# A planner's model of a shared PSUM bank, of DMA landing and of a shared port is altered, and its shifts are drawn anew

## The chip, the cores and the metric

The kernel runs on one core of one Trainium2 chip. The metric is the device time of one execution in microseconds (us). The engines are PE (matrix multiply), DVE (VectorE), ACT (ScalarE), POOL (GpSimd) and SP, which here only issues DMAs. Each engine works through its own instructions strictly in their order and waits for the others through semaphores.

## The reference, cut to what matters

```python
# attention, 4 batches, 8 heads, 1152 keys, head size 64; q pooled in pairs: 576 queries
q_pool = q.reshape(B, H, S // 2, 2, D).mean(axis=3)
scores = scale * np.matmul(q_pool, k.transpose(0, 1, 3, 2))
attn = np.exp(scores - np.max(scores, axis=-1, keepdims=True))
attn = attn / (np.sum(attn, axis=-1, keepdims=True) + 1e-09)
x = np.matmul(attn, v)                       # -> 2304 tokens x 512
# first feed-forward layer, 512 -> 2048 -> 512, a rational function between
h = x @ w_in
g = (a[0] + a[1]*h + a[2]*h*h + a[3]*h*h*h) / (1 + abs(b[0])*abs(h) + abs(b[1])*h*h + 1e-6)
x = g @ w_out
# second layer: one of 8 experts for each token, 512 -> 1024 -> 512
e_idx = np.argmax(x @ w_gate, axis=1)
out[mask] = gate_w * sigmoid * (np.maximum(x[mask] @ w1[e], 0.0) @ w2[e])
```

## The kernel before

Every float32 operand is split into a high and a low float16 part, and a product is three matmuls. The work runs in two stages. In the second, the experts' slots of 128 tokens are written out by hand in a fixed order; the diff does not touch it. In the first, a **planner** (`Plan`) sets the order. The code calls `plan.add` for every step with a key (its wanted place), the engines that may do it with a cost in us for each, and the names that it reads and writes. `Plan.order` then places all steps one after another on a model of the five engines: at each turn it takes, over all engines, the ready step with the earliest start (ties go by key), and so it decides both the order on each engine and, where two engines may do a step, which one does. `SHIFT` holds a number for each kind of step that is added to its key; `BIAS` and `PEN` hold numbers that make an engine dearer for steps with a choice. A kind ends in "." for the start of the program and in "!" for its end. The program that comes out has the fixed order; the costs exist only in the model.

Attention is done in 144 units of 128 query rows each (one head, or two heads of half a tile). Unit n goes through these steps: the scores for keys 0 to 1023 into the PSUM tile `sab` and those for the last 128 keys into a part of the PSUM tile `shared` (L828, PE; L825 for half tiles); the maximum over `sab` (L838, DVE) and over the rest (L841, DVE, called mc in the code); the exponent's bias (L848 on ACT or L850 on DVE, a step with a choice); the two exponentials (L856, ACT); the high part of the result (L865 on ACT or L867 on DVE), the low part (L871, mostly POOL); a transpose of both by DMA (L873, SP) into one of two buffers `pt`; the product with v into another part of `shared` (L880, PE). After four units a short chain on DVE reads the sums (L635) and writes the result out of `shared` (L909). The tile `shared` is one PSUM bank: the scores' rest, the products, and small sums across partitions lie in it side by side.

18 tiles of 128 tokens then go through the first feed-forward layer in four groups each: 48 matmuls with w_in (L1172 to L1174), the rational function on ACT, DVE and POOL (L1183 to L1206), 12 with w_out (L1213 to L1215). A chain of small steps chooses the expert (`route`). Before all that, both weight matrices are loaded as 8-byte numbers (L971), made float32 on DVE (L974 to L981), scaled and split (L1028, L651). `chain` adds each small instruction on DVE as a step of its own; `scale_of` makes the exponent's scale and `gate` the token's weight, each beginning with an instruction that reads two SBUF operands.

The model in `Plan.order` knows: for a step with `bank` on `shared`, PE waits until readers have finished and readers wait until PE has; for a step with `port`, DVE and POOL exclude each other; a DMA's result is ready when its modelled transfer ends plus `LAT["SP"]`.

Of the kernel before, what the change touches and what calls it, by code (L numbers as in the profile page):

```python
# [21 lines left out]
SHIFT = {'X/PE': -98.7,
 'X/PE.': -1.1,
 'bias/DVE+ACT': 54.5,
 'bias/DVE+ACT!': -16.9,
 'bias/DVE+ACT.': 35.7,
 'chain cf/DVE': -8.9,
 'chain cf/DVE.': 22.0,
 'chain den/DVE': -3.4,
 'chain den/DVE!': -27.4,  # L30
 'chain den/DVE.': -30.2,
 'chain esc/DVE': 53.8,
 'chain esc/DVE!': -67.3,
 'chain esc/DVE.': -212.0,
 'chain ps/DVE': 37.4,
 'chain ps/DVE!': 3.7,
 'chain qsc/DVE': -65.4,
 'chain qsc/DVE.': 3.5,
 'chain ro/DVE': 1.0,
 'chain ro/DVE!': -13.3,  # L40
 'chain rt/DVE': -12.9,
 'chain rt/DVE!': 0.1,
 'chain sc/DVE': 0.5,
 'chain sc/DVE.': -4.9,
 'chain wsi/DVE.': -4.5,
 'chain wso/DVE.': -0.9,
 'chain xm/DVE': 18.4,
 'chain xm/DVE.': 25.9,
 'chain xs/DVE': 44.6,
 'chain xt/DVE': -9.5,  # L50
 'chain xt/DVE.': -97.6,
 'chain yg/DVE': 0.5,
 'chain yg/DVE!': -1.3,
 'const/DVE.': -42.6,
 'cwld/SP.': 49.7,
 'first/DVE': 6.5,
 'firstn/DVE': 20.6,
 'gh/ACT': -36.3,
 'gh/ACT!': 0.1,
 'gh/DVE': -20.5,  # L60
 'gl/DVE': -68.3,
 'gl/DVE!': -44.3,
 'gw/DVE': 4.9,
 'gw/SP': 35.1,
 'h/ACT': -231.3,
 'h/DVE': 18.2,
 'h/PE': -0.1,
 'h/PE.': 306.2,
 'kT/SP': -4.3,
 'kT/SP.': 229.4,  # L70
 'kr/SP': 91.6,
 'kr/SP.': -7.0,
 'krB/SP.': 182.2,
 'line/PE': 40.5,
 'line/PE.': 23.8,
 'mab/DVE': 62.8,
 'mab/DVE!': -18.0,
 'mab/DVE.': -42.5,
 'mc/DVE': -1.1,
 'mc/DVE!': -113.7,  # L80
 'mc/DVE.': 242.3,
 'mk/ACT': -19.4,
 'mk/ACT.': 6.6,
 'mk/DVE': 3.3,
 'most/PE': 3.4,
 'most/PE.': -63.0,
 'mv/DVE': 28.4,
 'mv/DVE.': -28.4,
 'mxi/DVE.': -105.4,
 'mxo/DVE.': 23.3,  # L90
 'nB/DVE+ACT.': 4.9,
 'nBl/DVE+POOL.': -79.2,
 'nrm/DVE+ACT': -24.2,
 'nrm/DVE+ACT.': -145.8,
 'nrmQ/DVE': 7.3,
 'nrmQ/DVE+ACT': 291.9,
 'nrmQl/DVE+POOL': 101.6,
 'nrmQl/DVE+POOL.': 43.8,
 'nrml/DVE+POOL': -5.1,
 'nrml/DVE+POOL.': -100.6,  # L100
 'oacc/POOL+DVE': -226.7,
 'oacc/POOL+DVE!': 167.8,
 'p/ACT': 127.7,
 'p/ACT!': 31.0,
 'p/ACT.': 109.5,
 'pad/SP': 13.0,
 'pad/SP.': -32.6,
 'padded/SP!': 8.8,
 'pads/SP': 86.8,
# [1 line left out]
 'pc/ACT!': -7.3,
 'pc/ACT.': -4.2,
 'ph/DVE': -0.9,
 'ph/DVE+ACT': 5.4,
 'ph/DVE+ACT!': 272.0,
 'pl/POOL+DVE': -9.0,
 'pl/POOL+DVE!': 6.3,
 'pl/POOL+DVE.': -68.5,
 'pt/SP': 1.2,
 'pt/SP!': -1.0,  # L120
 'pt/SP.': -37.0,
 'pv/PE': -51.8,
 'pv/PE!': 179.5,
 'pv/PE.': -4.0,
 'qT/SP': -24.6,
 'qm/DVE': -2.4,
 'qm/DVE.': 28.7,
 'qr/SP': -18.8,
 'qr/SP.': 2.3,
 'qs/DVE+POOL': 4.0,  # L130
 'qs/DVE+POOL.': 58,
 'raw/SP.': -2.4,
 'rawz/SP!': -120.8,
 're/ACT': -4.0,
 're/ACT!': 25.6,
 'rs/ACT': 56.2,
 'rs/ACT!': -2.3,
 'run/DVE': 38.7,
 'run/DVE!': 13.4,
 'sab/PE': -56.3,  # L140
 'sab/PE!': 69.2,
 'sab/PE.': 6.8,
 'scr/DVE.': -36.5,
 'sq/ACT.': 79.7,
 'sq/DVE': -5.5,
 'sum/PE': -19.2,
 'sum/PE!': 6.6,
 'sum/PE.': 2.8,
 'tab/DVE!': 27.1,
 'th/ACT': 5.7,  # L150
 'th/ACT!': -126.8,
 'th/DVE': -41.8,
 'tp/DVE': 26.6,
 'tp/POOL+DVE': 1.9,
 'tp/POOL+DVE!': -21.6,
 'tq/ACT': -3.5,
 'tq/ACT!': -95.6,
 'tq/DVE': 4.3,
 'tw/DVE': 54.6,
 'tw/DVE!': -77.7,  # L160
 'vh/DVE+ACT': -79.8,
 'vh/DVE+ACT.': -29.3,
 'vl/DVE+POOL': -12.4,
 'vl/DVE+POOL.': -29.5,
 'vr/SP': 11.2,
 'vr/SP.': 435.7,
 'vrB/SP.': 27.7,
 'wih/ACT+DVE.': 27.9,
 'wil/POOL+DVE.': -0.9,
 'wm/DVE!': -3.5,  # L170
 'woh/ACT+DVE.': 610.7,
 'wol/POOL+DVE.': -13.5,
 'wp/DVE!': 20.1,
 'wq/DVE!': 4.3,
 'xT/DVE': 83.2,
 'xT/SP': 85.5,
 'xT/SP!': 5.2,
 'xT/SP.': -14.1,
 'xh/DVE': 1.3,
 'xh/DVE+ACT': -66.3,  # L180
 'xh/DVE+ACT!': 72.5,
 'xh/DVE+ACT.': -8.4,
 'xhf/DVE': -23.3,
 'xl/POOL+DVE': 3.6,
 'xl/POOL+DVE!': 16.3,
 'xl/POOL+DVE.': 79.8,
 'xr/DVE': -1.8,
 'xr/DVE!': -26.4,
 'xr/DVE.': 15.4,
 'xr/POOL.': 9.0,  # L190
 'y/PE': 83.3,
 'y/PE!': 37.1,
 'y/PE.': 78.5,
 'yT/DVE': -71.4,
 'yT/DVE+ACT': -2.9,
 'yT/DVE+ACT!': 128.8,
 'yr/ACT': -227.4,
 'yr/ACT!': -8.8,
 'ysort/POOL': 10.7,
 'ysort/POOL!': -92.5,  # L200
 'yt/POOL': 34.7,
 'yt/POOL!': 0.6,
 'yz/PE': 24.1,
 'yz/PE!': 18.9,
 'zh/ACT+DVE!': 0.6,
 'zhh/ACT!': 40.0,
 'zhl/DVE!': 20.2,
 'zl/DVE+POOL!': 57.5,
 'zm/DVE!': 16.3,
 'zob/ACT!': 1.8,  # L210
 'zout/POOL!': -0.7,
 'zr/SP!': -54.0,
 'zs/DVE!': -152.9,
 'zxT/SP!': 2.2,
 'zxh/ACT+DVE!': 49.6,
 'zxl/DVE!': 8.6}
BIAS = {('bias/DVE+ACT', 'ACT'): -1,
 ('bias/DVE+ACT', 'DVE'): -1,
 ('bias/DVE+ACT!', 'ACT'): -0.7,
 ('bias/DVE+ACT.', 'ACT'): 0.26,  # L220
# [49 lines left out]
 ('vl/DVE+POOL.', 'POOL'): 140.95,  # L270
 ('wih/ACT+DVE.', 'ACT'): 3.52,
 ('wih/ACT+DVE.', 'DVE'): 38.15,
 ('wil/POOL+DVE.', 'DVE'): 1.13,
 ('wil/POOL+DVE.', 'POOL'): 45.06,
 ('woh/ACT+DVE.', 'ACT'): 2.54,
 ('woh/ACT+DVE.', 'DVE'): 23.85,
 ('wol/POOL+DVE.', 'DVE'): -0.82,
 ('xh/DVE+ACT', 'ACT'): 6.14,
 ('xh/DVE+ACT', 'DVE'): 142.52,
 ('xh/DVE+ACT!', 'ACT'): -0.87,  # L280
 ('xh/DVE+ACT!', 'DVE'): 13.33,
 ('xh/DVE+ACT.', 'ACT'): 1.59,
 ('xh/DVE+ACT.', 'DVE'): 32.01,
 ('xl/POOL+DVE', 'POOL'): 163.04,
 ('xl/POOL+DVE!', 'DVE'): -0.95,
 ('xl/POOL+DVE!', 'POOL'): 85.78,
 ('xl/POOL+DVE.', 'DVE'): 33.11,
 ('xl/POOL+DVE.', 'POOL'): 1.33,
 ('yT/DVE+ACT', 'ACT'): 47.8,
 ('yT/DVE+ACT', 'DVE'): -1,  # L290
 ('yT/DVE+ACT!', 'ACT'): -0.38,
 ('yT/DVE+ACT!', 'DVE'): 10.2,
 ('zh/ACT+DVE!', 'ACT'): 30.31,
 ('zh/ACT+DVE!', 'DVE'): -0.62,
# [1539 lines left out]
```

## Time and profile before

| | us |
|---|---|
| runs | 1262.81, 1266.67, 1269.29 (median 1266.67) |
| profiled execution, its own time | 1264.07 |
| its span, first to last instruction | 1262.2 |
| PE busy | 984.2 (78%) |
| DVE busy | 925.8 (73%) |
| ACT busy | 866.6 (69%) |
| POOL busy | 634.8 (50%) |

The mean granted clock of PE over the span is 0.922. Busy shares are means over very different stretches: the first 112 us are loads and conversion of weights, from about 173 to 950 us attention and the first layer run side by side, and from about 1085 us on only the second stage is left.

### The profile page before, as it was taken

Reading aid. Unit: us, or ns where it says so; the run is one execution under the profiler, and the core shown is the slowest. Engines: PE = TensorE matmul, PEld = TensorE weight load, DVE = VectorE, ACT = ScalarE, POOL = GpSimd, SP = SyncE. Lnnn points to the kernel's source line nnn. Section 1 sums busy time; section 2 is a strip of 40 time slices with the busy share of each in tenths; the row PEclk is TensorE's granted clock in tenths of the full one; section 3 lists DMA queues with packets and bytes.
Section 4 is the critical chain, followed back from the end, with each engine's and each line's share of the span. In section 5 each row is a group of like instructions: output and inputs, shape, how many; then the busy total and the mean of one; then the engine's idle time right before and its main releaser. Section 6 shows DMA issues by size and latency. Waiting matters only on the chain. (4 is left out here: it accounts for less than half of the span.)

```text
span 1262.2 us, 30785 instructions
## 1 busy us (share of the span) xinstructions
PE 984.2 (78%) x12212; PEld 690.9 (55%) x12213; DVE 925.8 (73%) x1950; ACT 866.6 (69%) x1326; POOL 634.8 (50%) x413
## 2 busy tenths in 40 slices
PE   0124567878778888878878887988998799899986
PEld 0002345656455565555556655766666686677763
DVE  6797856777997977889878789877777894233354
ACT  3347678988678988877888987999898561122213
POOL 0105767566576755866766774776576200000000
PEclk9966689989889999998989998999899899999988
DMA  8986699769689968687987988897765621323351
GB/s 311 250 260 137 137 189 169 125 132 194 141 156 213 165 130 154 133 184 147 174 158 132 167 181 155 152 210 129 122 109 92 189 56 51 84 74 78 77 174 29
DMA packets 493097, 186.84 MB, mean 148 GB/s; under 512 B 454179, under 2 KB 472611, under 8 KB 492836
## 3 DMA queue, kind: packets, MB, share of 16 engines
q1 hardware_dynamic: 489972, 175.22, 69.6%
q0 software_dynamic: 2960, 9.46, 2.1%
q8 instruction: 99, 1.62, 0.5%
q14 instruction: 66, 0.54, 0.1%
HBM read 61.41 MB, written 12.88 MB: 59 GB/s over the span
## 5 line engine op out<-in xcount | busy, mean ns | idle before, releaser
L871 POOL TENSOR_TENSOR att<-att 128x1152 f16<-128x1152 f32 x96 | 232.0, 2418 | 122.7 <-ACT att L865 107.1
L1172 PE MATMUL hps<-scr,winh 128*128 128x128 f16 x1152 | 216.2, 225 | 23.4 <-DVE scr L1187 19.7
L1173 PE MATMUL hps<-scr,winh 128*128 128x128 f16 x1152 | 216.3, 225 | 0.0
L1174 PE MATMUL hps<-scr,winl 128*128 128x128 f16 x1152 | 216.2, 225 | 0.0
L838 DVE TENSOR_REDUCE small<-sab 128x1 f32<-128x1024 f32 x144 | 175.3, 1218 | 54.5 <-PE sab L828 40.4
L880 PE MATMUL shared<-att 128*128 128x65 f16 (+3 forms) x4320 | 159.0, 202 | 69.4 <-DMA att<-att 46.8
L880 PEld LDWEIGHTS <-att 128*128 128x128 f16 (+1 forms) x4320 | 147.8, 106 | 103.5 <-DMA att<-att 60.9
L1187 POOL TENSOR_TENSOR scr<-scr 128x512 f32<-128x512 f32 x135 | 176.3, 1307 | 52.1 <-ACT scr L1193 28.9
L856 ACT ACTIVATE att<-sab,small 128x1024 f32<-128x1024 f32 x144 | 173.9, 1209 | 0.5
L828 PE MATMUL sab<-att 128*128 128x512 f16 x512 | 146.2, 415 | 12.2 <-ACT att L856 9.2
L828 PEld LDWEIGHTS <-att 128*128 128x128 f16 x768 | 74.1, 105 | 128.4 <-issue 73.2
L1173 PEld LDWEIGHTS <-winh 128*128 128x128 f16 x1152 | 116.2, 101 | 38.5 <-issue 26.1
L1183 DVE SCALAR_TENSOR_TENSOR scr<-scr,small,hps 128x512 f32<-128x512 f32 x144 | 106.6, 740 | 31.8 <-ACT hps L1197 16.4
L1172 PEld LDWEIGHTS <-winh 128*128 128x128 f16 x1152 | 117.4, 102 | 19.8 <-issue 4.3
L871 POOL TENSOR_TENSOR scr<-att,scr 128x1152 f16<-128x1152 f32 x39 | 95.1, 2439 | 47.6 <-ACT scr L865 39.9
L1174 PEld LDWEIGHTS <-winl 128*128 128x128 f16 x1152 | 116.5, 101 | 0.0
L1213 PE MATMUL yps<-wouth,scr 128*128 128x512 f16 x288 | 111.7, 388 | 2.3 <-ACT small L1332 2.2
L1486 PE MATMUL sab<-att 128*128 128x128 f16 x608 | 107.8, 223 | 6.4 <-ACTq L1737 3.4
L1215 PE MATMUL yps<-wouth,scr 128*128 128x512 f16 x288 | 111.6, 387 | 0.8 <-DVE small L635 0.5
L1214 PE MATMUL yps<-woutl,scr 128*128 128x512 f16 x288 | 111.7, 388 | 0.0
L1488 PE MATMUL sab<-att 128*128 128x128 f16 x608 | 107.7, 223 | 3.9 <-DVEq L1737 3.2
L1510 POOL DMA_INDIRECT out_dram<-att x19 | 18.8, 990 | 179.2 <-ACTq L1737 92.2
(211 smaller groups left out, 2440.2 us busy)
## 6 DMA issues: line engine op xcount, KB each, us to landing
att<-in_k_dram SPq DMA_DIRECT2D x16, 576.0 KB, 4.5
att<-in_q_dram SPq DMA_DIRECT2D x16, 512.0 KB, 4.5
att<-in_moe_w_dram SPq DMA_DIRECT2D x4, 2048.0 KB, 8.2
att<-in_v_dram SPq DMA_DIRECT2D x14, 576.0 KB, 4.0
woutl<-in_moe_w_in_dram SPq DMA_DIRECT2D x10, 512.0 KB, 9.6
woutl<-in_moe_w_out_dram SPq DMA_DIRECT2D x10, 512.0 KB, 4.4
att<-ysort SPq DMA_DIRECT2D x19, 257.0 KB, 2.7
wouth<-in_moe_w_in_dram SPq DMA_DIRECT2D x6, 512.0 KB, 6.4
```

The source lines that it names most:

```text
L828: T.matmul(dst[:, d0:d0 + w], qT[:, H * x + 2 * i + t, :], rhs, start=(x == 0), stop=(x == 1))
L838: A(key - ahead - .6, {"DVE": 1.13}, lambda e: V.reduce_max(mm[:, 0, bi:bi + 1], ab, axis=AX.X), r=[f"sab{par}"] + mt, w=[f"mab{n}"] + ([f ...
L856: return lambda e: S.activation(dst, src, AF.Exp, bias=mm[:, 2, bi:bi + 1], scale=esc[:, 0, i:i + 1])
L871: lambda e: eng(e).tensor_tensor(out=phs[pb][:, 1], in0=p32, in1=ph(), op=SUB),
L880: T.matmul(pvb[p0:p0 + w, bi, 0:d], pt[:, lhs, p0:p0 + w], rhs[:, h, c, :], start=(c == 0 and lhs == 0 and rhs is vh), stop=(lhs == 2 * KC ...
L1172: T.matmul(hp, wh, xh[:, kc, :], start=(kc == 0), stop=False)
L1173: T.matmul(hp, wh, xl[:, kc, :], start=False, stop=False)
L1174: T.matmul(hp, wl, xh[:, kc, :], start=False, stop=(kc == KD - 1))
L1187: return lambda e: eng(e).tensor_tensor(out=out_, in0=i0, in1=i1, op=op)
L1213: T.matmul(yps, a, wouth[:, ff, :], start=(ff == 0), stop=False)
L1214: T.matmul(yps, a, woutl[:, ff, :], start=False, stop=False)
L1215: T.matmul(yps, b_, wouth[:, ff, :], start=False, stop=(ff == KF - 1))
```

## The change

The model is altered in five places. A step on the shared bank now starts only when every other engine's steps on it, in the order in which the planner places them, have ended (one owner at a time, readers of two engines included). A DMA's result is ready 1.15 us after its modelled end, not 0.6. The chains `scale_of` and `gate` are marked as users of the port. The cost of mc is 0.27, not 0.35. In `TU` the penalties for steps with a choice go from 1.999 to 0 on DVE (`pd`), from 0 to 0.367 on ACT (`pa`) and from 1.53 to 0.548 on POOL (`pp`). With that, all of `SHIFT` and `BIAS` have new numbers. No step's arithmetic differs; the two programs issue the same steps in another order and, for steps with a choice, partly on another engine.

```diff
- 'pc/ACT': -110.8,
+ 'pc/ACT': -53.6,
...
- ('bias/DVE+ACT', 'ACT'): -1,
- ('bias/DVE+ACT', 'DVE'): -1,
+ ('bias/DVE+ACT', 'ACT'): 77.89,
+ ('bias/DVE+ACT', 'DVE'): 0.24,
...
-    LAT = {"PE": 0.2, "DVE": 0.14, "ACT": 0.17, "POOL": 0.08, "SP": 0.6}
+    LAT = {"PE": 0.2, "DVE": 0.14, "ACT": 0.17, "POOL": 0.08, "SP": 1.15}
...
-        dma = read_end = write_end = 0.0
+        dma, banked = 0.0, dict.fromkeys(engines, 0.0)
...
                     if ops[i][6]:
-                        s = max(s, read_end if e == "PE" else write_end)
+                        s = max([s] + [banked[x] for x in engines if x != e])
...
             if o[6]:
-                if e == "PE":
-                    write_end = max(write_end, end + self.LAT[e])
-                else:
-                    read_end = max(read_end, end + self.LAT[e])
+                banked[e] = end + self.LAT[e]
...
-    def chain(key, fn, r=(), w=(), after=(), bank=0):
+    def chain(key, fn, r=(), w=(), after=(), bank=0, port=0):
...
-              w=[f"esc{r}_{i}" for i in range(c.start, c.stop)])
+              w=[f"esc{r}_{i}" for i in range(c.start, c.stop)], port=1)
...
-        A(key - ahead - .4, {"DVE": 0.35},
+        A(key - ahead - .4, {"DVE": 0.27},
...
-        chain(key + .15, gate, r=[f"rs{o}", f"re{o}", "yr"], w=["yg"])
+        chain(key + .15, gate, r=[f"rs{o}", f"re{o}", "yr"], w=["yg"], port=1)
```

Line numbers of the changed kernel are smaller by 6 in the rows below (its L867 is L873 of before, L844 is L850, L835 is L841, L832 is L838, L965 is L971, L874 is L880).

**The SP queue near the end of the weights' loads.** `woutl` and `wouth` serve as buffers for the raw w_out here; L658 are transposes of k, and L873 those of a unit's exponentials. Before:

```order
L971 DMA woutl<-in_moe_w_out_dram 128x1024 x2
L658 DMA_TRANSPOSE att<-att 128x18x128
L971 DMA wouth<-in_moe_w_out_dram 128x1024 x2
L971 DMA woutl<-in_moe_w_out_dram 128x1024 x4
L971 DMA wouth<-in_moe_w_out_dram 128x1024 x2
L971 DMA woutl<-in_moe_w_out_dram 128x1024 x2
L665 DMA att<-in_k_dram 128x2x576
L658 DMA_TRANSPOSE att<-att 128x18x128
L873 DMA_TRANSPOSE att<-att 128x18x128 x2
L667 DMA att<-in_v_dram 128x2x576
```

And now:

```order
L965 DMA wouth<-in_moe_w_out_dram 128x1024 x2
L867 DMA_TRANSPOSE att<-att 128x18x128
L965 DMA woutl<-in_moe_w_out_dram 128x1024 x2
L711 DMA att<-in_q_dram 128x8x128
L965 DMA woutl<-in_moe_w_out_dram 128x1024 x2
L652 DMA_TRANSPOSE att<-att 128x18x128
L867 DMA_TRANSPOSE att<-att 128x18x128
L652 DMA_TRANSPOSE att<-att 128x8x128
L867 DMA_TRANSPOSE att<-att 128x18x128 x2
L965 DMA wouth<-in_moe_w_out_dram 128x1024 x2
L867 DMA_TRANSPOSE att<-att 128x18x128
L965 DMA woutl<-in_moe_w_out_dram 128x1024 x2
```

The last loads of w_out stood ahead of the first unit's transpose; now five transposes of units stand between them, and the queue is in order.

**DVE in the middle of the run**, some units with a group of the first layer among them. Before:

```order
L841 TENSOR_SCALAR small<-shared,small 128x128
L1187 TENSOR_TENSOR scr<-hps_78,scr 128x512
L838 TENSOR_REDUCE small<-sab_75 128x1
L867 CAST att<-att 128x1152
L841 TENSOR_SCALAR small<-shared,small 128x128
L635 SCALAR_TENSOR_TENSOR small<-shared,small 128x4
L635 RECIPROCAL small<-small 128x4
L838 TENSOR_REDUCE small<-sab_74 128x1
L909 TENSOR_TENSOR att<-shared,small 128x256
L1183 SCALAR_TENSOR_TENSOR scr<-scr,small,hps_77 128x512
L841 TENSOR_SCALAR small<-shared,small 128x128
L850 TENSOR_SCALAR small<-small 128x1
```

And now:

```order
L629 TENSOR_SCALAR small<-shared 128x1
L629 TENSOR_SCALAR small<-small 128x1 x2
L1177 SCALAR_TENSOR_TENSOR scr<-scr,small,hps_78 128x512
L835 TENSOR_SCALAR small<-shared,small 128x128
L844 TENSOR_SCALAR small<-small 128x1
L832 TENSOR_REDUCE small<-sab_74 128x1
L1177 SCALAR_TENSOR_TENSOR scr<-scr,small,hps_78 128x512
L835 TENSOR_SCALAR small<-shared,small 128x128
L1321 COPY scr<-yps 128x512
L844 TENSOR_SCALAR small<-small 128x1
L1181 TENSOR_TENSOR hps_78<-scr,hps_78 128x512
```

Before, three maxima L841 stand here with one bias L850; the other biases were on ACT. Now each L835 is followed one or two rows later by an L844, the bias, on DVE. Over the program DVE has 120 of the 144 biases, and had 42.

**PE ahead of the product of unit 130.** Before, with the scores of unit 133 (`sab`) and four transposes of the router ahead of it:

```order
L880 MATMUL shared<-att 128x65
L828 LDWEIGHTS att
L828 MATMUL sab_75<-att 128x512
L828 LDWEIGHTS att
L828 MATMUL sab_75<-att 128x512
L828 LDWEIGHTS att
L828 MATMUL sab_75<-att 128x512
L828 LDWEIGHTS att
L828 MATMUL sab_75<-att 128x512
L1324 MATMUL yps<-ident,yr 128x128 x4
L880 LDWEIGHTS att
L880 MATMUL shared<-att 128x65
```

And now, where the scores up to unit 136 and more groups of the first layer (the last rows of one stand first here) have been placed ahead of the same product:

```order
L1167 LDWEIGHTS winh
L1167 MATMUL hps_78<-scr,winh 128x128
L1168 LDWEIGHTS winl
L1168 MATMUL hps_78<-scr,winl 128x128
L1292 LDWEIGHTS tri
L1292 MATMUL yps<-oh_89,tri 128x8
L1293 LDWEIGHTS ones_82
L1293 MATMUL yps<-oh_90,ones_82 128x8
L874 LDWEIGHTS att
L874 MATMUL shared<-att 128x65
L874 LDWEIGHTS att
L874 MATMUL shared<-att 128x64
```

The product of unit 130 has moved down past PE work of later units and of the first layer.

## Rows read from the trace of the kernel before

**Rows 1.** The view by windows: columns as in its first line.
```profile
core 0: us, PE busy (x) PEld busy (x) DVE busy (x) ACT busy (x) POOL busy (x), PEclk, DMA share, GB/s
0.00:112.00 112.00, 24.15 (x63) 7.56 (x64) 89.78 (x169) 49.05 (x53) 19.79 (x19) 0.85 0.83 243
112.00:173.00 61.00, 33.40 (x408) 21.65 (x408) 44.13 (x91) 41.80 (x53) 42.24 (x22) 0.64 0.87 171
173.00:950.00 777.00, 648.67 (x8700) 459.75 (x8693) 630.31 (x1357) 665.55 (x1058) 523.67 (x329) 0.94 0.85 156
950.00:1085.00 135.00, 120.70 (x1360) 89.00 (x1359) 95.64 (x211) 68.02 (x115) 33.55 (x27) 0.95 0.39 94
1085.00:1262.00 177.00, 157.26 (x1694) 112.96 (x1692) 65.95 (x125) 42.21 (x50) 15.59 (x17) 0.95 0.33 85
```

**Rows 2.** Who waited for whom on PE, 173 to 950: total us, times, longest us.
```profile
PE shared L880 <- DMA att<-att: 34.6, 26, 3.4
...
PE shared L828 <- ACT att L856: 18.4, 19, 2.0
...
PE shared L880 <- DMA att<-scr: 18.0, 9, 6.4
```

**Rows 3.** Timeline of PE: two products that waited.
```profile
249.52 1.00 PE L880 MATMUL shared<-att 128*128 128x65 f16 x27 [0.76 <-DMA att<-att]
...
899.66 1.00 PE L880 MATMUL shared<-att 128*128 128x65 f16 x27 [2.14 <-DMA att<-att]
```

**Rows 4.** The SP queue's own waits, whole run, same columns.
```profile
SPq L873 <- PE shared L880: 49.5, 24, 7.6
```

**Rows 5.** DMA issues: count, median us from issue to landing.
```profile
att<-att SPq DMA_TRANSPOSE x137, 4.8
...
att<-scr SPq DMA_TRANSPOSE x62, 5.3
```

**Rows 6.** Who waited for whom on DVE, 173 to 950.
```profile
DVE small L635 <- ACT att L856: 3.9, 6, 1.0
...
DVE att L909 <- ACT att L856: 3.5, 5, 1.4
```

**Rows 7.** Who waited for whom on ACT, 173 to 950.
```profile
ACT small L848 <- DVE small L841: 25.4, 23, 4.2
...
ACT att L856 <- DVE small L635: 7.5, 8, 1.9
```

**Rows 8.** Groups by line and form: count, busy us, mean ns, idle before.
```profile
L841 DVE TENSOR_SCALAR_CACHE_REDUCE small<-shared,small 128x128 bf16<-128x128 f32 x144 | 49.7, 345 | 34.0 <-PE shared L828 15.5 <-PE shared L880 14.9 <-PE shared L825 1.6
...
L635 DVE SCALAR_TENSOR_TENSOR small<-small 128x1 f32<-128x1 f32 x18 | 12.7, 706 | 0.6 <-ACT small L1335 0.3 <-ACT small L1332 0.2
...
L841 DVE DVE_READ_ACCUMULATOR small<-shared,small 128x1 f32 x144 | 11.8, 82 | 0.0
...
L850 DVE TENSOR_SCALAR small<-small 128x1 f32<-128x1 f32 x42 | 8.8, 209 | 0.7
...
L635 DVE SCALAR_TENSOR_TENSOR small<-small 128x2 f32<-128x2 f32 x16 | 8.5, 538 | 0.0
...
L635 DVE SCALAR_TENSOR_TENSOR small<-shared,small 128x4 f32<-128x4 f32 x36 | 5.6, 155 | 7.7 <-PE shared L880 5.2 <-ACT att L856 2.4 <-PE shared L828 0.2
...
L848 ACT ACTIVATE small<-small 128x1 f32<-128x1 f32 x102 | 40.0, 392 | 34.8 <-DVE small L841 34.4
```

**Rows 9.** Timeline of the start, DVE, SP and PE: start us, us.
```profile
99.26 0.34 DVE L841 TENSOR_SCALAR_CACHE_REDUCE small<-shared,small 128x128 bf16<-128x128 f32 x1
...
90.42 0.80 SPq L971 DMA_DIRECT2D woutl<-in_moe_w_out_dram  x2
...
109.23 6.12 SPq L873 DMA_TRANSPOSE att<-att  x2
...
173.22 0.22 PE L1172 MATMUL hps<-scr,winh 128*128 128x128 f16 x1
...
173.83 0.22 PE L1174 MATMUL hps<-scr,winl 128*128 128x128 f16 x1
```

More of the change, by code (lines that the diff above doesn't have):

```diff
@@ L20 @@
 EARLY, LATE = 9.0, 128.0
 DIGITS = str.maketrans("", "", "0123456789_")
[L22 to L109, printed above, removed]
- 'pc/ACT': -110.8,
[L111 to L216, printed above, removed]
@@ new lines @@
+BIAS = {('bias/DVE+ACT', 'ACT'): 77.89,
+ ('bias/DVE+ACT', 'DVE'): 0.24,
+ ('bias/DVE+ACT!', 'ACT'): -0.45,
+ ('bias/DVE+ACT!', 'DVE'): 12.76,
+ ('bias/DVE+ACT.', 'ACT'): 0.32,
+ ('bias/DVE+ACT.', 'DVE'): 1.41,
+ ('nB/DVE+ACT.', 'ACT'): 0.08,
+ ('nBl/DVE+POOL.', 'DVE'): 0.17,
+ ('nBl/DVE+POOL.', 'POOL'): 0.18,
+ ('nrm/DVE+ACT', 'ACT'): 1.76,
+ ('nrm/DVE+ACT', 'DVE'): 25.14,
+ ('nrm/DVE+ACT.', 'ACT'): 0.89,
+ ('nrm/DVE+ACT.', 'DVE'): 26.67,
+ ('nrmQ/DVE+ACT', 'ACT'): -1,
+ ('nrmQ/DVE+ACT', 'DVE'): 1.05,
+ ('nrmQ/DVE+ACT.', 'ACT'): 0.53,
+ ('nrmQ/DVE+ACT.', 'DVE'): 22.22,
+ ('nrmQl/DVE+POOL', 'DVE'): -0.26,
+ ('nrmQl/DVE+POOL', 'POOL'): 7.4,
+ ('nrmQl/DVE+POOL.', 'POOL'): 1.32,
+ ('nrml/DVE+POOL', 'DVE'): -0.24,
+ ('nrml/DVE+POOL', 'POOL'): 0.36,
+ ('nrml/DVE+POOL.', 'DVE'): 215.85,
+ ('nrml/DVE+POOL.', 'POOL'): 62.52,
+ ('oacc/POOL+DVE', 'DVE'): 0.23,
+ ('oacc/POOL+DVE', 'POOL'): 28.29,
+ ('oacc/POOL+DVE!', 'DVE'): -1,
+ ('oacc/POOL+DVE!', 'POOL'): 28.54,
+ ('ph/DVE+ACT', 'ACT'): 0.84,
+ ('ph/DVE+ACT', 'DVE'): 1.39,
+ ('ph/DVE+ACT!', 'ACT'): -0.16,
+ ('ph/DVE+ACT!', 'DVE'): -1,
+ ('ph/DVE+ACT.', 'ACT'): -1,
+ ('ph/DVE+ACT.', 'DVE'): -0.11,
+ ('pl/POOL+DVE', 'DVE'): -0.16,
+ ('pl/POOL+DVE', 'POOL'): -0.86,
+ ('pl/POOL+DVE!', 'DVE'): 0.14,
+ ('pl/POOL+DVE!', 'POOL'): -0.85,
+ ('pl/POOL+DVE.', 'DVE'): 20.08,
@@ L270 @@
[L270 to L294, printed above, removed]
+ ('qs/DVE+POOL', 'POOL'): 10.94,
+ ('qs/DVE+POOL.', 'DVE'): 16.01,
+ ('qs/DVE+POOL.', 'POOL'): 1.08,
+ ('tp/POOL+DVE', 'DVE'): 72.64,
+ ('tp/POOL+DVE', 'POOL'): 0.04,
+ ('tp/POOL+DVE!', 'DVE'): 91.92,
@@ new lines @@
+ ('tp/POOL+DVE!', 'POOL'): -0.71,
+ ('vh/DVE+ACT', 'ACT'): -0.36,
+ ('vh/DVE+ACT', 'DVE'): -1,
+ ('vh/DVE+ACT.', 'ACT'): -1,
+ ('vh/DVE+ACT.', 'DVE'): -0.25,
+ ('vl/DVE+POOL', 'DVE'): -0.69,
+ ('vl/DVE+POOL', 'POOL'): 26.85,
+ ('vl/DVE+POOL.', 'DVE'): 3.38,
+ ('vl/DVE+POOL.', 'POOL'): 30.08,
+ ('wih/ACT+DVE.', 'ACT'): 0.79,
+ ('wih/ACT+DVE.', 'DVE'): 134.86,
+ ('wil/POOL+DVE.', 'DVE'): 0.14,
+ ('wil/POOL+DVE.', 'POOL'): 0.56,
+ ('woh/ACT+DVE.', 'ACT'): 50.03,
+ ('woh/ACT+DVE.', 'DVE'): 54.51,
+ ('wol/POOL+DVE.', 'POOL'): 0.85,
@@ new lines @@
+ ('xh/DVE+ACT', 'ACT'): -0.02,
+ ('xh/DVE+ACT', 'DVE'): -1,
+ ('xh/DVE+ACT!', 'ACT'): 0.04,
+ ('xh/DVE+ACT!', 'DVE'): -0.25,
+ ('xh/DVE+ACT.', 'ACT'): 20.05,
+ ('xh/DVE+ACT.', 'DVE'): 9.23,
+ ('xl/POOL+DVE', 'DVE'): -0.3,
+ ('xl/POOL+DVE', 'POOL'): 0.27,
+ ('xl/POOL+DVE!', 'DVE'): -0.96,
+ ('xl/POOL+DVE!', 'POOL'): -0.26,
+ ('xl/POOL+DVE.', 'DVE'): -0.42,
+ ('xl/POOL+DVE.', 'POOL'): 7.01,
+ ('yT/DVE+ACT', 'ACT'): 0.43,
+ ('yT/DVE+ACT', 'DVE'): 35.84,
+ ('yT/DVE+ACT!', 'ACT'): 25.21,
+ ('yT/DVE+ACT!', 'DVE'): 2.34,
@@ L295 @@
+ ('zh/ACT+DVE!', 'ACT'): -1,
+ ('zh/ACT+DVE!', 'DVE'): 1.33,
  ('zl/DVE+POOL!', 'DVE'): -1,
- ('zl/DVE+POOL!', 'POOL'): 40.87,
- ('zxh/ACT+DVE!', 'ACT'): -0.31}
+ ('zxh/ACT+DVE!', 'ACT'): 0.01}
 class Plan:
-    LAT = {"PE": 0.2, "DVE": 0.14, "ACT": 0.17, "POOL": 0.08, "SP": 0.6}
+    LAT = {"PE": 0.2, "DVE": 0.14, "ACT": 0.17, "POOL": 0.08, "SP": 1.15}
     PEN = {"PE": 0.0, "DVE": TU["pd"], "ACT": TU["pa"], "POOL": TU["pp"], "SP": 0.0}
@@ L636, in chain @@
                      r=list(r) + ([name + str(x - 1)] if x else []), w=[name + str(x)] + (list(w) if last else []),
-                     after=list(after) + list(w) if x == 0 else (), kind="chain " + list(w)[0].translate(DIGITS), bank=bank)
+                     after=list(after) + list(w) if x == 0 else (), kind="chain " + list(w)[0].translate(DIGITS), bank=bank, port=port)
     def hi(out_, in_, sc):
```

240 lines of the change are left out of this document (190 added, 50 removed).

## The prediction

> **What bounds the kernel now.** I read the view by windows first, then who waited for whom on each engine in the long middle stretch, then the groups by line. In [rows 1] the reader is to see that no engine is full in any stretch. PE's work is the same in both programs, so the time is PE's busy time plus PE's idle time. PE's idle time is 87.9 us up to 112 us (112 less 24.15), 27.6 up to 173, 128.3 up to 950, 14.3 up to 1085 and 19.7 after. The last stretch is not touched. The first is bound by loads and by DVE, which converts the weights (89.8 of 112 us). So a gain must come from the 128.3 us in the middle or from the two stretches before it. In the middle PE is busy 648.7 of 777 us, DVE 630.3, ACT 665.6: three engines between 81 and 86%, which wait for each other in turn. The longest of PE's waits there is for the DMA transpose ahead of a unit's product with v: 34.6 and 18.0 us in 35 waits, 1.5 us each; next is 18.4 us for ACT's exponential to leave `shared` [rows 2].
>
> **Term 1, the later landing.** A transpose takes 4.8 us from issue to landing in the median, 5.3 from the second buffer area [rows 5]. The model counted 1.35 + 2.65 + 0.6 = 4.6 from the issue when the queue is free; now 5.15. So the old plan placed products too early by a few tenths, and the new one about right. What that does is read from the order: for each of the units 24 to 135 I add up PE's matmuls between the end of its scores and its product, at 55.5 ns for 128 columns (twelve matmuls from 173.22 to 173.83 [rows 9]). Before it is 14.8 us in the mean, now 16.35. The products' waits of before, from the one at 249.52 to that at 899.66 [rows 3], 47.3 us for these 112 units, sort by that amount: 22 units under 12 us waited 0.77 us in the mean, 20 between 12 and 14 waited 0.44, 32 to 16 waited 0.38, 22 to 18 waited 0.28, 16 above waited 0.20. The new order has 7, 21, 31, 21 and 32 units in these classes, which makes 38.7 us: **-8.6 us**. Below, a shift of 1.6 us ends each of the 35 waits of 1.5 us: -52.6. Above, a later product frees its `pt` buffer later, and 24 transposes already waited 49.5 us on the queue for that [rows 4]: 24 x 1.6 = +38 if all of it came back to PE.
>
> **Term 2, one owner of the bank.** DVE and ACT wait for each other at `shared` though both only read: DVE's chains and results 3.9 and 3.5 us for ACT's exponential [rows 6], ACT 7.5 us for DVE's chains [rows 7]; together 14.9 us, which the old model did not know. The Trainium skill says the same: PSUM — Partial Sum Buffer, section "PSUM bank collisions raise a hardware error", reports that the compiler back end makes any two instructions on different engines that touch one bank and quadrant depend on each other, ScalarE against VectorE and read against read included. By that rule the term is a gain; if readers could share the bank, it would be nothing or a loss. The waits stand in both programs; only the plan has learned of them. In the new order 22 of DVE's instructions on `shared` wait on ACT, before 27: -14.9 x 5/27 = -2.8. Against it, the score matmuls that wait on ACT go from 111 to 118: +18.4 x 7/111 = +1.2. **-1.6 us**, with bounds -14.9 and +1.2.
>
> **Term 3, work that changes engines.** The 144 biases: ACT had 102 at 392 ns, DVE 42 at 209 ns [rows 8]; now 24 and 120. That is -30.6 us on ACT and +16.3 on DVE. The other steps with a choice, counted in the same way by their lines, come to about +2 on ACT, -7 on DVE (nine additions less, among others) and +6 on POOL. Net: ACT -28, DVE +9. The fullest engine of the middle, ACT at 665.6, comes to about 637, DVE to 639, and PE with 648.7 is now the fullest: at most 17 us for the fullest. ACT's own waits of 25.4 us for L841 [rows 7] are not a gain, since the exponential still waits for that maximum. With no engine over 86%, I take a third: **-5 us**, bounds -28 (all of ACT's) and +9 (all of DVE's).
>
> **Term 4, the port.** The instruction that opens `scale_of` (128x2) takes 538 ns and that of `gate` (128x1) 706 ns, both with two SBUF operands; the same form that reads `shared` takes 155 [rows 8]. The excess is 16 x 0.383 + 18 x 0.551 = 16 us of DVE. The Trainium skill, SBUF — State Buffer, section "Who interferes with whom", has it that a DVE instruction with two SBUF inputs is shut out for a whole GpSimd instruction, not slowed in share; the trace's 706 against 155 ns agrees. By the rule the wait stays what it is unless the plan finds POOL idle, and POOL gets 6 us more work; so it gives little, as the rows do. The stalls lie beside PE work: **-1 us**, bounds -16 and 0.
>
> **Term 5, the start.** Before, the last w_out load is issued at 90.42, the first unit's transpose at 109.23, the first L841 runs at 99.26 and the first group's matmul at 173.22 [rows 9]. In the new order DVE reaches the first L835 after fewer conversions, and the first units run between them; 16 units' worth of products, not 12, stand before the first group. That fills DVE's idle time from 112 to 173, which is 16.9 us [rows 1]. But the last two loads of w_out stand behind five transposes, 3.06 us of queue each (6.12 for two [rows 9]): +15 us, if they hold up the first layer's coefficients, which need both weights. I take **-6 us**, about a third of the idle time, bounds -17 and +15.
>
> **Term 6, the end.** Behind the last product PE has 48 matmuls of the first layer more, 48 x 0.0555 = 2.7 us, in a stretch where ACT and DVE are half idle: **+1 us**, bounds 0 and +2.7.
>
> **Sum.** -8.6 - 1.6 - 5 - 1 - 6 + 1 = -21. Terms 1 to 3 shorten the same idle time of PE, and where one wait goes the next releaser is often late by nearly as much; I keep two thirds: -14. Against the profiled execution's own 1264.07 this gives **1250 us**. That execution lies 0.2% under the median of the runs, 1266.67. A measurement of this kernel can tell about 0.5% (6 us) from no change.
>
> **Rivals.**
> *DVE falls behind the plan and sets the pace (slower).* The plan now prices the maximum of the last 128 keys at 0.27 us; its rows say 345 + 82 = 427 ns [rows 8]. The unpriced part grows from 0.077 to 0.157 us, over 144 units by 11.5 us; 78 more biases at 0.135 in the plan and 0.209 in the row add 5.8; with the 9 us of added work, DVE is later by 26 than the plan thinks. It stood idle 19% of the middle, so half may be absorbed: +13, 1277 us. It decides once DVE is busy above about 86% of the middle, where ACT is now; for it speaks that DVE gets the work, against it that 639 of 777 is 82%.
> *No change.* Both orders were found on a model, the waits only move: the releasers of PE's 128 us are many, and the largest are 34.6, 18.4 and 18.0 [rows 2]. With term 5 at zero the terms come to -15; if two thirds of that are given back elsewhere, the time is 1264 - 5 = 1259.
> *The start costs.* If the w_out loads come 15 us later and the first group with them, less the 8.6 of term 1: 1270 us. It decides if the first L1172 (now L1166) runs later than 173 us while no more products have been done by then.
> *The waits at the products vanish.* Half of the 52.6 us goes and the start fills all 16.9: 1264 - 26 - 17 + 1, 1222 us. Against it speaks that 39 us of waits remain by the classes.
>
> **How the numbers follow.** The forecast, a gain of 7 to 30 us, 0.48; the products' waits vanishing, 0.07; no change 0.22; DVE's pace 0.16; the start's cost 0.07. Faster by over 0.5% is 0.48 + 0.07, same 0.22, slower 0.16 + 0.07. The likeliest one's own range is 1234 to 1257. The range for 8 in 10 reaches up to most of DVE's rival and down short of 1222: 1230 to 1276.
>
> **What would show it.** Right: PE's waits L874 <- DMA in the middle fall from 52.6 to about 44 us, its idle time there by 8 to 15 us; L842 on ACT (the bias) has 24 runs, ACT's busy time falls by about 28 us, DVE's rises by about 9; the first score maxima (L835) run before 85 us. Wrong: DVE's busy share of the middle above 86%, or waits of PE for DVE taking the place of those for DMA; SP's waits for PE at L867 growing by tens of us; the first group of the first layer starting after 173 us.

## The result and the profile after

The changed kernel takes **1226.88 us** in the median of 4 runs (1225.84 to 1232.98), against 1267.74 for the kernel before on the same chip: ratio 0.9687, 95% interval 0.9646 to 0.9727, 41 us less. The forecast of 1250 had the direction and a third of the size; the result lies 3 us below its range. The profiled execution took 1232.98 us, the longest of them, with a span of 1231.1, 31.1 under the span before; the rows below are from it. Line numbers are those of before less 6.

The windows, with the ends of the stretches moved to the same work ([rows 1] is the table before):

```profile
core 0: us, PE busy (x) PEld busy (x) DVE busy (x) ACT busy (x) POOL busy (x), PEclk, DMA share, GB/s
0.00:112.00 112.00, 31.89 (x156) 13.28 (x157) 86.60 (x161) 53.32 (x64) 37.56 (x29) 0.65 0.90 256
112.00:173.00 61.00, 35.07 (x521) 25.02 (x521) 57.12 (x110) 40.31 (x53) 22.18 (x12) 0.67 0.75 158
173.00:920.00 747.00, 635.35 (x8460) 453.33 (x8459) 623.26 (x1436) 638.04 (x966) 506.25 (x305) 0.94 0.88 162
920.00:1050.00 130.00, 117.62 (x1377) 85.78 (x1377) 85.79 (x208) 70.96 (x120) 60.58 (x45) 0.99 0.41 95
1050.00:1231.00 181.00, 160.65 (x1703) 115.41 (x1700) 66.73 (x127) 42.20 (x50) 16.38 (x18) 0.94 0.33 85
```

PE's busy time is the same to 4 us (980.6 against 984.2), so the gain is idle time of PE, 27 us of it, and most of that lies in the middle: 747 - 635.4 = 111.7 us, before 128.3. The granted clock there is 0.94 in both. DVE is busy 83.4% of the middle, ACT 85.4%.

What PE waits for from 173 to 920, as in [rows 2]:

```profile
PE shared L822 <- ACT att L850: 25.0, 22, 3.3
PE hps L1166 <- DVE scr L1181: 17.4, 19, 2.9
PE shared L874 <- DMA att<-att: 12.2, 11, 2.3
PE sab L822 <- ACT att L850: 9.1, 10, 1.9
...
PE shared L874 <- DMA att<-scr: 4.0, 6, 1.5
```

The products (L874) wait 16.2 us for transposes, where it was 52.6. Other waits have grown in return. The longest of PE's waits for DVE, now 17.4 us, was this one before:

```profile
PE hps L1172 <- DVE scr L1187: 12.4, 15, 2.1
```

Summed over the middle by what ended them, PE's waits for DMA fall from 55 to 18 us, and those for DVE rise from 30 to 48. The SP queue's waits for a product to free its buffer have grown as term 1 feared, from the 49.5 us and 24 times of [rows 4] over the whole run:

```profile
SPq L867 <- PE shared L874: 73.4, 40, 10.1
```

The groups by line that answer to [rows 8]: the bias on ACT (24 runs) and DVE (120), and the openers, as the first instructions of `scale_of` (128x2) and `gate` (128x1) are called here.

```profile
L842 ACT ACTIVATE small<-small 128x1 f32<-128x1 f32 x24 | 9.4, 390 | 17.7 <-DVE small L835 17.7
...
L844 DVE TENSOR_SCALAR small<-small 128x1 f32<-128x1 f32 x120 | 25.0, 208 | 1.3
...
L629 DVE SCALAR_TENSOR_TENSOR small<-small 128x2 f32<-128x2 f32 x16 | 4.2, 267 | 0.0
...
L629 DVE SCALAR_TENSOR_TENSOR small<-small 128x1 f32<-128x1 f32 x18 | 3.3, 186 | 0.7 <-ACT small L1329 0.7
```

The start, as the first instructions of a line (times: first and last start). It answers to [rows 9]:

```profile
L835 DVE TENSOR_SCALAR_CACHE_REDUCE small<-shared,small x2: 340/343/346, 77.4 to 85.3; 128x128 bf16<-128x128 f32 x2
...
L1166 PE MATMUL hps<-scr,winh x6: 287/314/314, 157.3 to 158.9; 128*128 128x128 f16 x6
```

The first maximum of last keys runs at 77.4 us (99.26 before), the first group at 157.3 (173.22). But unit 24's product starts at 246.9 us against 249.5: of 16 to 22 us at the start 3 are left there. From the start of unit 24's product to that of unit 135, divided by 111, the pace falls from 6.19 to 5.96 us a unit, 26 us in all. One milestone recurs below, the last matmul of the first layer's first line, the end of the planned middle. It is read from these two rows, before and after, at the second time of each:

```profile
L1172 PE MATMUL hps<-scr,winh x58: 216/219/312, 999.9 to 1031.8; 128*128 128x128 f16 x58
```

```profile
L1166 PE MATMUL hps<-scr,winh x60: 216/219/312, 969.8 to 997.7; 128*128 128x128 f16 x60
```

So **34.1 us** are won up to there: 3 before unit 24's product, 26 from there to unit 135's, 6 behind it. The tail, all that runs after the milestone, is 3 us longer (233.4 against 230.4).

Over units 24 to 135 the time fell by 26 us, and PE's waits at their products by 25 (47.3 to 22.0, whatever ended them; those for transposes from 46 to 14). That invites the reading that the waits at the products were the bound and the later landing took half of them away. The two numbers agree by chance, though: in this stretch PE's idle time fell by 19 us (111.9 to 93.0) and its busy time by 7 (575.6 to 568.9), so that part of what the products gained was lost at other waits. **Theory 1** is this reading. **Theory 2**: those waits only show where PE stands when something else is late; the gain lies in the order as a whole. Further rivals within it are the bias' engine (runs 3 and 4), and that a longer search alone, under any rules, gives the gain (runs 9 to 16).

### The profile page after: what moved, and what is told of

The parts are those of the page before. It is cut to its first block, busy times and chain, and to the rows that moved or that the text cites. A ratio compares the mean times of both kernels' runs of the same rounds, so it can differ in the third digit from the quotient of the medians.

```text
span 1231.1 us, 30781 instructions
## 1 busy us (share of the span) xinstructions
PE 980.6 (80%) x12213; PEld 692.8 (56%) x12213; DVE 919.5 (75%) x2038; ACT 844.8 (69%) x1250; POOL 643.0 (52%) x405
## 5 line engine op out<-in xcount | busy, mean ns | idle before, releaser
L1181 POOL TENSOR_TENSOR scr<-scr 128x512 f32<-128x512 f32 x144 | 191.7, 1332 | 70.4 <-ACT scr L1187 36.0
L832 DVE TENSOR_REDUCE small<-sab 128x1 f32<-128x1024 f32 x144 | 175.2, 1219 | 35.2 <-PE sab L822 25.6
L874 PE MATMUL shared<-att 128*128 128x65 f16 (+3 forms) x4320 | 158.6, 202 | 39.1 <-DMA att<-att 25.9
L874 PEld LDWEIGHTS <-att 128*128 128x128 f16 (+1 forms) x4320 | 147.1, 107 | 60.1 <-DMA att<-att 35.7
L850 ACT ACTIVATE att<-sab,small 128x1024 f32<-128x1024 f32 x144 | 175.5, 1220 | 2.3 <-DVE small L629 1.6
L865 POOL TENSOR_TENSOR scr<-att,scr 128x1152 f16<-128x1152 f32 x41 | 99.1, 2416 | 40.4 <-ACT scr L859 28.9
L1480 PE MATMUL sab<-att 128*128 128x128 f16 x608 | 109.7, 225 | 7.1 <-DMA att<-att 3.7
L1482 PE MATMUL sab<-att 128*128 128x128 f16 x608 | 109.6, 225 | 2.8 <-DVEq L1731 2.2
```

What stands on the lines that cost most here:

```text
L832: A(key - ahead - .6, {"DVE": 1.13}, lambda e: V.reduce_max(mm[:, 0, bi:bi + 1], ab, axis=AX.X), r=[f"sab{par}"] + mt, w=[f"mab{n}"] + ([f ...
L850: return lambda e: S.activation(dst, src, AF.Exp, bias=mm[:, 2, bi:bi + 1], scale=esc[:, 0, i:i + 1])
L865: lambda e: eng(e).tensor_tensor(out=phs[pb][:, 1], in0=p32, in1=ph(), op=SUB),
L874: T.matmul(pvb[p0:p0 + w, bi, 0:d], pt[:, lhs, p0:p0 + w], rhs[:, h, c, :], start=(c == 0 and lhs == 0 and rhs is vh), stop=(lhs == 2 * KC ...
L1181: return lambda e: eng(e).tensor_tensor(out=out_, in0=i0, in1=i1, op=op)
```

## The experiments

Ratios are to the kernel before, with 95% intervals.

**1 and 2. Products moved by hand.** In the written-out order of steps each product is moved past PE's steps until these come to 1.0 us by the plan's costs (before's order, down) or 1.6 us (the changed order, up). The last step passed may go beyond the limit. By the traces PE's matmuls between a unit's scores and its product (units 24 to 135, mean) go from 14.8 to 16.0 us and from 16.4 to 14.0. The edit, shortened:

```
+order = [(i, e) for _, i, e in self.order()]
+for v in products:
+    at = order.index((v, "PE"))
+    # past PE steps until 1.0 us in all; stops at a step that needs v and at the next product
...
+    order.insert(best + 1, order[at])
+    del order[at]
```

> The kernel before, with each product with v moved down in the finished order past up to 1.0 us of PE work (by the plan's own costs) that does not need it; the mean PE work between a unit's scores and its product grows by about 1.5 us, as between the two kernels. Theory 1 (the gain comes from products that stand later, behind their transposes' landing): PE's waits for DMA at the products fall from 52.6 us by 20 or more and the time by 15 to 25, to 1243 to 1253. Rival (work moved between ACT and DVE, or the rest of the order): within 6 us of before. A third outcome, slower, if products that come later only free their pt buffers later.

> The changed kernel, with each product moved up in the finished order past up to 1.6 us of PE work that it does not need; the mean PE work between scores and product falls by about 2.2 us, to less than before. Theory 1: PE's waits for DMA at the products grow from about 24 us back to 50 or more, and the time from 1227 to 1245 to 1255. Rival: within 6 us of 1227.

Measured: 1327.62 us, **1.048** [1.0429, 1.053], 60 us slower; and 1367.36, **1.0796** [1.0743, 1.0849]. The first is the third outcome named there; the second lies over 100 us above what either theory gave. The first is the telling one. Waits from 173 to 1000 us, PE's and the SP queue's (lines of before plus 13), and one line of before that [rows 2] leaves out:

```profile
PE sab L841 <- ACT att L869: 41.3, 47, 2.3
PE shared L841 <- ACT att L869: 28.6, 29, 3.5
...
PE shared L893 <- DMA att<-att: 2.6, 4, 1.4
...
PE shared L893 <- DMA att<-scr: 1.3, 2, 0.9
```

```profile
SPq L886 <- PE shared L893: 94.9, 47, 6.8
```

```profile
PE sab L828 <- ACT att L856: 7.1, 13, 1.3
```

The products' waits for transposes are gone, 3.9 us in place of 52.6, and the kernel is 60 us slower: the scores wait 69.9 us for the exponential instead (25.5 before), and the transposes 94.9 us for their buffers (49.5 before). A kernel can have almost no waits at the products and a worse pace. In the second run these waits are 79.7 us, more than in either kernel.

**3 and 4. The biases' engines exchanged**, each order kept step by step:

```
+by = iter("ADDADADA...")    # cut: the other kernel's choice, D or A for each of 144
+bias = {i: "ACT" if next(by) == "A" else "DVE" for i, o in enumerate(self.ops) if o[5].startswith("bias/")}
 for _, i, e in self.order():
-    self.ops[i][2](e)
+    self.ops[i][2](bias.get(i, e))
```

> The changed kernel in its own order, but each of the 144 biases on the engine that it had before (42 on DVE, 102 on ACT). Rival 2 (ACT's relief by 28 us is the gain): slower by 10 to 28 us, 1237 to 1255. Theory 1: slower by at most 8 us.

> The kernel before in its own order, but each bias on the engine that it has in the changed kernel (120 on DVE). Rival 2: faster by 10 to 28 us, 1240 to 1257. Theory 1: within 8 us of before.

Measured: the changed order with before's engines 1237.05, **0.978** [0.9731, 0.9829], 10 to 12 us worse than the changed kernel; before's order with the new engines 1269.58, **1.001** [0.9982, 1.0037]. The move is worth about 10 us in the order that was made for it and nothing in the other; it is not the gain of 41.

**5 and 6. Products that wait for no transpose.** Every step keeps its place; the products read a constant tile, so the attention's result is not the reference's. They then hold no buffer either, and a transpose no longer waits for them.

```
-T.matmul(pvb[p0:p0 + w, bi, 0:d], pt[:, lhs, p0:p0 + w], rhs[:, h, c, :],
+T.matmul(pvb[p0:p0 + w, bi, 0:d], ones16.bitcast(F16)[:, p0:p0 + w], rhs[:, h, c, :],
```

> Before's order, every instruction in its place, but the products with v read a constant tile in place of the transposed exponentials, so that they wait neither for a transpose to land nor hold its buffer (the transposes still run; the attention's result is not the reference's). Theory 1, the waits at the products set the pace of the middle: the 47.3 us of waits of units 24 to 135 go and little comes in their place, ratio to before 0.96 to 0.98 (25 to 50 us less). Theory 2, the pace is set by the other engines (ACT and DVE at 81 to 86%) and the products' waits only show it: PE waits as much elsewhere (scores for the exponential, sab for ACT), ratio 0.99 to 1.00.

> The same edit in the changed kernel's order: the products read a constant tile and wait for no transpose. Its waits there are 23.5 us. Theory 1: 10 to 24 us less than the changed kernel, ratio to before 0.95 to 0.96, so that the two orders come within 10 to 15 us of each other without these waits. Theory 2: under 6 us less than the changed kernel, and the difference of the two orders stays 30 us or more.

Measured: 1224.35, **0.9623** [0.9559, 0.9687], and 1187.29, **0.9347** [0.9292, 0.9402]: 41 us less each. But the two do not differ from their originals in the middle alone. The milestone, in before's order and in the changed one:

```profile
L1172 PE MATMUL hps<-scr,winh x47: 216/219/311, 989.7 to 1014.9; 128*128 128x128 f16 x47
```

```profile
L1166 PE MATMUL hps<-scr,winh x32: 217/219/219, 968.3 to 977.7; 128*128 128x128 f16 x32
```

Up to there 16.9 us are won in before's order and 20.0 in the changed one. The other 23 to 25 us are the tail, which has fewer matmuls to do there, since the routing follows from the attention's result; the first line of the tail's first product, before and in run 5:

```profile
L1486 PE MATMUL sab<-att 128*128 128x128 f16 x563 | 100.2, 223 | 5.6 <-ACTq L1737 3.4 <-DMA att<-att 2.2
```

```profile
L1486 PE MATMUL sab<-att 128*128 128x128 f16 x531 | 92.6, 221 | 3.4 <-ACTq L1737 3.4
```

So taking away all waits for transposes at the products (52.6 us in the middle) is worth 17 us in before's order, a third; and without these waits the two orders are still 1014.9 - 977.7 = **37.2 us** apart, not less than the 34.1 with them. By its size in before's order, 17 us, neither theory is right (25 to 50, or under 13). In the changed order the 20 us are what theory 1 expects, but its clause that the orders then come within 15 us of each other fails, and theory 2's, that the difference stays, holds. As the account of the difference between the two orders theory 1 is refuted.

**7 and 8. Rules without their numbers.** The new planner with before's three tables; and the changed kernel with one constant moved:

```
-    LAT = {"PE": 0.2, "DVE": 0.14, "ACT": 0.17, "POOL": 0.08, "SP": 1.15}
+    LAT = {"PE": 0.2, "DVE": 0.14, "ACT": 0.17, "POOL": 0.08, "SP": 1.10}
```

> The changed kernel's planner (later landing, one owner of the bank, port flags, 0.27 us) with before's TU, SHIFT and BIAS. If the gain lies in the rules themselves: ratio 0.97 to 0.99. If the numbers found anew carry it and any old numbers are fitted to the old rules: slower than before, 1.03 to 1.07 (the plan's own length goes from 993 to 1039 us).

> The changed kernel with the landing constant 1.10 in place of 1.15 us, nothing else: a control of how far an order depends on the tables' fit. If the orders depend smoothly on the constant: within 1% of the changed kernel (ratio 0.96 to 0.98). If the tables fit one order alone: slower than the changed kernel by 30 to 70 us, ratio 0.99 to 1.02 (the plan's own length goes from 967 to 1029 us).

Measured: 1282.17, **1.0107** [1.007, 1.0145]; and 1275.64, **1.006** [1.0032, 1.0088]. Better rules with old numbers are 1% slower than before (less than the 3 to 7% expected), and 0.05 us in one constant costs the changed kernel all of its gain (0.9687 to 1.006). The tables fit one order; a rule taken alone through the planner can't be judged so.

**9 to 16. Rules told apart by equal searches.** So the rules were compared in another way: from before's order, with the planner's lengths as the judge, the same 1.5 million trial moves of a step (past a few others, or to another engine) under different rules, and the order found is written into the kernel:

```
 def trace(self):
-    for _, i, e in self.order():
-        self.ops[i][2](e)
+    # cut: imports, the five engines' names, and above the class the text ORDER
+    code = zlib.decompress(base64.b85decode(ORDER))
+    for x in range(0, len(code), 2):
+        i, e = divmod(code[x] + 256 * code[x + 1], 5)
+        self.ops[i][2](names[e])
```

> Before's order, improved step by step (1.5 million trial moves of one step past a few others or to another engine, kept when the plan's own length does not grow) under before's rules: the plan's length falls from 993 to 931 us under the old rules, and stays at 1044 (1042 before) under the new ones. Theory 1, a longer search alone gives the gain: ratio 0.95 to 0.98. Theory 2, the rules give it, since before's order is already fitted to the old ones and more fitting to them is empty: ratio 0.99 to 1.02.

> The same improvement from the same order with the same number of trials, but under all of the new rules: the plan's length under them falls from 1042 to 938 us. Theory 1 (search): the same ratio as the run under the old rules, within 0.01. Theory 2 (rules): ratio 0.95 to 0.975, as the changed kernel or better.

> The same improvement from before's order under before's rules with one of the new ones, the later landing (1.15 for 0.6 us). If the landing carries the gain, as term 1 of the forecast has it: ratio 0.96 to 0.98, and the products' waits for DMA fall by half or more. If it is another rule: 0.99 to 1.01.

> The same improvement under before's rules with the port flags of the two short chains and the 0.27 us of the last keys' maximum, and nothing else of the new. By term 4 of the forecast (1 us) next to nothing: ratio 0.99 to 1.01. By the plan's replay of before's order, in which this rule alone adds 26 us (landing 21, bank 16), it carries a good part: 0.96 to 0.98.

> As the first improvement under the old rules (ratio 0.9858), with another row of random moves. If that result is the rules': ratio 0.98 to 0.992. If one search says little: outside this, as far as 0.965 or 1.0.

> As the first improvement under all new rules (ratio 0.9655), with another row of random moves. If that result is the rules': 0.96 to 0.972, at least 0.01 under the search with the old rules and the same moves. If it was luck: 0.975 or more.

> As the first improvement with the later landing alone (ratio 0.9733), with another row of random moves. If the landing is worth 10 us over a search with the old rules: 0.968 to 0.979. If that was luck: 0.98 to 0.99, as under the old rules.

> The same improvement from before's order under before's rules with the one owner of the bank and nothing else of the new. If the bank's rule carries what the landing does not (all new rules gave 13 us more than the landing alone): ratio 0.97 to 0.98. If it is worth the 1.6 us of the forecast's term 2: 0.98 to 0.99, as under the old rules.

Measured; the last column is the milestone (1031.8 before, 997.7 in the changed kernel):

| search under | moves | median us | ratio | milestone us |
|---|---|---|---|---|
| before's rules | first | 1245.45 | 0.9858 [0.9806, 0.9909] | 1006.6 |
| before's rules | second | 1249.16 | 0.9870 [0.9813, 0.9927] | 998.3 |
| and the port and 0.27 us | first | 1250.32 | 0.9864 [0.9807, 0.9921] | 1007.2 |
| and one owner of the bank | first | 1246.72 | 0.9827 [0.9774, 0.9879] | 1004.3 |
| and the later landing | first | 1234.62 | 0.9733 [0.9685, 0.9780] | 993.6 |
| and the later landing | second | 1222.82 | 0.9658 [0.9605, 0.9711] | 987.1 |
| all new rules | first | 1221.16 | 0.9655 [0.9614, 0.9697] | 978.9 |
| all new rules | second | 1216.59 | 0.9597 [0.9542, 0.9651] | 975.1 |

Search under unchanged rules gives 1.4% (0.9864 in the mean of two), about 17 us. The later landing adds 1.7% (mean 0.9696), about 21 us. All rules together reach 0.9626, 9 us more. The port's rule gives nothing alone; the bank's gives 5 us, within the intervals. Of the two theories that run 9 set against each other neither came: there is slack left under the old rules, and the rules give more than the search.

How firm are these steps? Two searches under one set of rules differ by up to 0.75% (9 us), and so the step from the old rules to the landing, between whose ratios there is a gap of at least 1.25%, is not one search's luck; the 9 us from the landing to all rules are no larger than that scatter. The milestones, of one execution each, divide the gain in another way: 29 us for the search, 12 for the landing, 13 for the rest, with tails of 238 us in the mean under all three (230 before). So the landing is worth 12 to 21 us. Taken alone it is the largest of the rules; that it is worth more than the others together is not shown.

Where PE waits at the products in these kernels, 173 to 930 us (lines of before plus 102): first the old rules, then the later landing, then all rules (the first search of each):

```profile
PE shared L982 <- DMA att<-att: 12.5, 11, 2.2
PE yps L1400 <- DVE oh L737: 7.9, 5, 3.5
PE shared L982 <- DMA att<-scr: 7.3, 7, 2.7
```

```profile
PE shared L982 <- DMA att<-att: 20.4, 18, 2.1
...
PE shared L982 <- DMA att<-scr: 7.9, 5, 2.3
```

```profile
PE shared L982 <- DMA att<-att: 15.0, 15, 4.6
...
PE shared L982 <- DMA att<-scr: 4.3, 4, 3.1
```

The first search with the old landing has 19.8 us of these waits, the one with the new landing 28.3, and the second is 11 us faster. In the second searches it is 20.5 and 15.7; the means are 20 and 22. The landing rule's worth does not show at the products. It hardly shows in how long a product stands behind its landed transpose (units 24 to 135, mean): 2.1 us in both searches under the old rules, 2.4 with the later landing; in the kernel before it was 1.2, in the changed one 2.5. From issue to landing it is 5.4 to 5.6 us in all of them.

Summed by releaser from 150 us to the last product, PE's waits for DVE are 79 and 63 us under the old rules, 64 and 60 with the landing, 53 and 49 with all; those for DMA 25 and 23, 32 and 24, 25 and 19. From the old rules to all of them the saving is thus mostly where PE waits for DVE. That is no price either: with the bank's rule alone these waits are 51 us too, and the kernel gains nothing clear by it. Nor is it how the change itself came out: from the kernel before to the changed one the waits for DMA fall from 60 to 26 and those for DVE rise from 36 to 55.

**17 and 18. From the changed order on.** The same search from the changed order under its rules; then, from what it found, 4 million more trials with 392 and 209 ns for the bias and 427 for the last keys' maximum, as [rows 8] has them.

> The changed kernel's order, improved in the same way under its own rules (1.5 million trials; the plan's length falls from 967 to 926 us). The search from before's order gave a plan of 938 and 943 us and ratios of 0.9655 and 0.9597. If the plan's length orders the kernels: faster than the changed kernel by 15 to 30 us, ratio 0.945 to 0.957. If the rest is noise below what the rules know: 0.96 to 0.97.

> The previous order, improved further (4 million trials) with the measured 392 and 209 ns of the bias and 427 ns of the last keys' maximum in the plan. If these errors matter as the landing's did: 5 to 15 us under the previous run, ratio 0.94 to 0.95. If not: within 5 us of it.

Measured: 1228.42, **0.9678** [0.9615, 0.9741], the changed kernel's time, though the plan counts 41 us less; and 1204.44, **0.9483** [0.9428, 0.9538], 2% under the changed kernel and the fastest of those that do all of the work. In the first result the plan's length no longer orders kernels this close: 926 us in the plan here, 938 and 943 in the two searches under all rules above, which are faster. The second has truer prices and more trials at once; which of them gave the 24 us is not told apart.

## Why the prediction was wrong

**The step that failed is "Term 1, the later landing: -8.6 us", in its method.** It valued the rule by the products' waits, sorted by PE's work between scores and product. The waits fell to 16.2, not to 44, so the classes did not foretell them. Sorted in the same way, the 28 units of the changed kernel with less than 14 us of such work wait 2 us in all, where the classes of before give 15; and a search under the old rules has 19.8 us of these waits with no change of the landing. Run 1 has 16.0 us of such work, nearly as much as the changed kernel with its 16.4, and is 60 us slower than before. Nor were the waits the price: without any of them before's order gains 17 us of the 52.6, and the gap of the two orders stays. The landing rule, which the prediction had at 8.6, is worth 12 to 21 us in the equal searches all the same, by waits that lie elsewhere.

**A term was missing.** The sum went rule by rule, as if both orders were equally well fitted. A search under before's own rules takes 17 us, more than the whole forecast gain of 14. In the equal searches it is 17 of 47 us (29 of 55 at the milestone); how much of the changed kernel's 41 us it is can't be told from its trace.

**"I keep two thirds"** discounted in the wrong direction. The terms were taken as overlapping; the result is more than their whole sum of 21 (31 in the profile, 41 in the medians).

*Term 2* (-1.6): the bank's rule alone gave 5 us in the searches, not told from zero. The Trainium skill, PSUM — Partial Sum Buffer, section "PSUM bank collisions raise a hardware error", has it that the compiler makes readers on two engines depend on each other too; this fits the waits of ACT and DVE in [rows 6, 7]. That the planner knows of it has shown no price of its own here.

*Term 3* (-5): ACT's busy time fell by 21.8 us (28 foretold), the 24 runs on ACT and 390 and 208 ns are as read. Worth: 10 us, with the new order. DVE's busy time did not rise by 9 but fell by 6, since term 4 gave it back more.

*Term 4* (-1): of the two things said, that the stalls stay and that they are worth little, the first is wrong. 18 x (706 - 186) + 16 x (538 - 267) = 13.7 us of DVE went, near the bound of -16. A kernel does not need this to be fast: in run 18, the fastest that does all of the work, the openers of `gate` and `scale_of` take 474 and 504 ns.

```profile
L737 DVE SCALAR_TENSOR_TENSOR small<-small 128x1 f32<-128x1 f32 x18 | 8.5, 474 | 0.1
...
L737 DVE SCALAR_TENSOR_TENSOR small<-small 128x2 f32<-128x2 f32 x16 | 8.0, 504 | 0.0
```

What the 13.7 us are worth in the changed order was not tried by itself; in the search with the port's rule alone these openers still take 528 and 500 ns (597 and 784 in the first search under the old rules), so that run prices the rule and not the stalls. The Trainium skill, SBUF — State Buffer, section "Who interferes with whom", has such an instruction shut out for a whole GpSimd instruction. The trace agrees, as the last section shows: 145 to 159 ns when POOL runs nothing at its start, and otherwise mostly the rest of POOL's instruction.

*Term 5* (-6): the first maximum came before 85 us as foretold (77.4; the second at 85.3), the first group 16 us earlier; at unit 24 3 us are left. *Term 6* (+1): 3.

**The rivals.** DVE did not set the pace (83.4%, bound 86%). "No change" and "the start costs" did not occur. "The waits at the products vanish", 1222 us at 0.07, has nearly the time, but by luck: the waits did vanish by two thirds, but they are worth a third of themselves, and the start that was to give 17 us gave 3. Two of the signs of being wrong came as well, and in a faster kernel: the queue's waits for PE grew by 24 us, and in the middle PE's waits for DVE grew by 18 where those for DMA fell by 37.

What stays open: by which waits the later landing gains its 12 to 21 us, and how the changed kernel's 41 us divide between rules and fitting.
